# Products with v in float16 parts for the second piece of an attention and MLP kernel, with weight conversions queued two units earlier

## The chip, the cores and the metric

The kernel runs on one core of a Trainium2 chip. The metric is device time in microseconds (us) of one execution. Five engines with queues of their own work side by side: TensorE (PE) multiplies matrices out of the on-chip memory into accumulation banks, VectorE (DVE) and ScalarE (ACT) work element by element, GpSimd (POOL) does a little of that, and SyncE (SP) issues transfers (DMA). Each engine takes its instructions in the order of its queue. An instruction whose input isn't there holds up all that stands behind it.

## What is computed

The input is q, k and v for 2 batches, 8 heads, 768 positions and 64 dimensions a head. Attention keeps a window of 128 positions and 4 sinks at the start. Its output goes through a normalised two-layer network, and that through a gated mixing stage, which the change leaves alone.

```
scores = scale * q @ k.T                  # masked: first n_sink keys, or 0 <= pos_q - pos_k < window
a = exp(scores - max); a = a / sum(a)
x = a @ v                                 # heads side by side: (2, 768, 512)
xn = (x - mean) / sqrt(var + 1e-6) * g
x = x + relu(xn @ w_ch1) @ w_ch2          # w_ch1: 512 x 2048, w_ch2: 2048 x 512
theta = x @ w_theta                       # then cos, sin, two token mixes, a last product with relu
```

## The kernel before

The 1536 rows are cut into six pieces of two tiles of 128 rows (tiles, L482): pieces 0 to 2 are batch 0, pieces 3 to 5 batch 1. attn_fast (L275) is a generator that goes through pieces and heads, and stops (yield) between small groups of products, so that run (L820) can set other work of TensorE between them.

For each head softmax (L379) forms the scores (L273), subtracts from the mask with the row's extreme on DVE (L394), and takes the exponential with its sum on ACT (L397). A tile sees two blocks of 128 keys (its own and the one before) and, from the third tile of a batch on, 16 columns of sinks. For the product with v the weights must be transposed, and there are two ways. Pieces 0 and 1 (TURNED is 2) are transposed on TensorE, in float32: turn_w (L433) transposes the blocks into one bank, wp, and copies them out into wt, by ACT in even heads (L449), by DVE in odd ones (L447); turn_sinks (L452) transposes the sink columns of the next head into a free half of the bank pv, and DVE copies them to ws (L458); values (L460) multiplies with v in float32 (L477), one head after its transposes, and normalize (L494) scales the result out of pv into x. Bank pv is a single one here, and so is bank wp from unit 0 on. Later pieces split the weights into two float16 parts (send_w, L402: high part on ACT, rest on DVE), which a transfer transposes. With v in two float16 parts too, a block takes three products: high x high, high x low, low x high. Three groups of 16 rows stand in one product for the sinks.

v comes in two forms. whole_v (L200) loads a tile in float32 as it is, for pieces 0 and 1. split_v (L181) loads a tile to a buffer vr, of which there is one, writes the high part on ACT (L196, for the sinks' tile L190) and the rest on DVE (L198). The pool for v holds five tiles. load_v (L286) asks for a piece's tiles while the piece before is in work, but for piece 2 only at the end of piece 1.

The network runs in units: unit u is the 128 hidden rows of one block of weights, u modulo 16, for all pieces that take part. first (L641) is the product with w_ch1, then the relu on ACT (L651, from unit 8 on L674); second (L679) is the product with w_ch2 into acc (L696). Piece 0 starts at unit 0, piece 1 joins at unit 8. Units 0 to 7 use float32 (L649); from unit 8 on x and the weights are each split into two parts on ACT and DVE (L637, L638; x in norm_T, L625 and L626).

The weights come as 64-bit numbers. load_w12 (L569) loads the two blocks of unit f (512 KB each) and load64 (L546) makes float32 of each: L555 on DVE, L556 and L558 on ACT, L559 on DVE. There are four buffers for the raw numbers, so that the load of f waits for the conversion of f-2. Conversions of f=0 to 3 are placed in the first piece. For the others run has this loop, where `newest` and behind() put all that load_w12 gives to ACT behind the relu of unit u in ACT's queue:

```
while f < NF and f <= u + AHEAD[u >= OFF - 1]:
    self.newest = [self.relu[u]]
    with self.behind():
        self.load_w12(f)
```

With AHEAD (2, 3) f=4 stands behind the relu of unit 2, f=8 behind that of unit 6, f=9 and f=10 behind that of unit 7, f=11 behind that of unit 8. TensorE's order is the program's own (manual_schedule); the other queues are ordered at build time by a planner that works with estimated durations, and the first two pieces' transposes, products and normalisations have high priority in it. range_whole (L206) at the end of attention loads once more those tiles of v that were never split, for a check of their range.

Of the kernel before, what the change touches and what calls it, by code (L numbers as in the profile page):

```python
# [8 lines left out]
F32 = mybir.dt.float32  # L9
F32R = mybir.dt.float32r  # L10
F16 = mybir.dt.float16
# [10 lines left out]
NT = S // 128  # L22
# [30 lines left out]
AHEAD = (2, 3)  # L53
# [16 lines left out]
class Net:  # L70
# [110 lines left out]
    def split_v(self, b, t):  # L181
# [6 lines left out]
        if t == NT:  # L188
            o = p["v"].tile([128, DM], F16, tag="vk", name="vk", bufs=1)
            nc.scalar.activation(o, r, AF.Copy, scale=VSC)  # L190
            r, lo, hi = r[64:96], o[64:96], o[64:96]
            self.v3[b, t] = o
        else:
            o = p["v"].tile([128, 2, DM], F16, tag="v", name="v")
            hi, lo = o[:, 0], o[:, 1]
            nc.scalar.activation(hi, r, AF.Copy, scale=VSC)  # L196
            self.v3[b, t] = hi, lo
# [77 lines left out]
    def attn_fast(self, eng):  # L275
# [10 lines left out]
        def load_v(piece):  # L286
            if piece < NP:
                b, tiles = self.tiles(piece)
                if piece < TURNED:
                    for t in tiles:  # L290
                        self.whole_v(b, t)
                    return
# [6 lines left out]
        def turn():  # L299
# [3 lines left out]
            with ahead(piece):  # L303
                blocks = self.turn_w(pt, tiles, h)
            sinks = []
            if tiles[0]:
                p["ws"].append(p["ws"].pop(0))
                sinks = [p["ws"][-1][0:NSK, i] for i in range(PIECE)]
# [30 lines left out]
        for j, (piece, h) in enumerate(steps):  # L339
# [4 lines left out]
            if h == (3 if piece else V_NEXT) and piece != TURNED - 1:  # L344
                load_v(piece + 1)
            pt, st = yield from self.softmax(h, tiles, qk[piece, h])
# [4 lines left out]
            if piece < TURNED and h == H - 1:  # L351
# [8 lines left out]
                if piece == TURNED - 1:  # L360
                    load_v(piece + 1)
# [17 lines left out]
    def softmax(self, h, tiles, qk):  # L379
# [19 lines left out]
        self.inverse(st, PSC * VSC if qk[1] is not None else 1.0)  # L399
# [33 lines left out]
    def turn_w(self, pt, tiles, h):  # L433
# [7 lines left out]
        for x, (i, t) in enumerate(keys):  # L441
            c0 = (t + 1 - tiles[i]) * KW
            nc.tensor.transpose(ps[:, x * 128:(x + 1) * 128], pt[:, i, c0:c0 + 128], self.ident)  # L443
        wt = self.att["wt"].tile([128, m, 128], F32, tag="wt", name="wt")
        ps = ps[:, 0:m * 128].rearrange("p (m k) -> p m k", k=128)
# [6 lines left out]
    def turn_sinks(self, bank, pt, sinks):  # L452
# [5 lines left out]
        nc.vector.tensor_copy(self.att["ws"][-1][0:NSK], ps)  # L458

    def values(self, b, h, tiles, piece, blocks, sinks, st, after):  # L460
# [6 lines left out]
        for i in range(len(tiles)):  # L467
            if piece < TURNED:
                prods = [(a, self.whole[b, t][:, hc]) for (j, e, t), a in blocks.items() if j == i]
                if sinks:  # L470
                    prods.append((sinks[i], self.whole[b, 0][0:NSK, hc]))
            else:
                prods = [(a, v[:, hc]) for (j, e, t), a in blocks.items() if j == i for v in self.v3[b, t][:2 - e]]
                if sinks:
# [345 lines left out]
    def run(self, general):  # L820
# [27 lines left out]
        else:  # L848
# [6 lines left out]
            a["ws"] = [ws.tile([128, PIECE, 128], F32, name=f"ws{i}") for i in range(2)]  # L855
# [243 lines left out]
```

## Time and profile before

| | |
|---|---|
| runs shown | 617.91, 623.66, 625.28 us; median 623.66 |
| the profiled execution | 617.65 us, span 615.9 us |
| TensorE busy | 584.7 us, 95% |
| DVE, ACT, POOL busy | 408.5, 334.0, 60.1 us |
| granted clock of TensorE, mean | 0.983 |
| transfers | 56.4 MB, 32% of the DMA engines' time |

The profile is of one execution, and its own time (617.65 us) lies near the lowest of the runs. Busy time of TensorE counts from a matmul's start to its modelled end, and matmuls overlap; what a group of them costs on the path is read from the chain of waits. The granted clock is a share of the full 2.4 GHz. An idle time stands in brackets behind the instruction that ended it, with the engine and line that the profile takes for its cause.

### The profile page before, as it was taken

The numbers are of one execution on the slowest core, as the hardware profiler recorded it, in microseconds if no ns is written. First come the engines' busy times: TensorE is split into PE (matmuls) and PEld (weight loads), VectorE is DVE, ScalarE is ACT, GpSimd is POOL, SyncE is SP. The second block draws the span as 40 slices with busy tenths as digits, with TensorE's granted clock in tenths as the row PEclk, the third lists the DMA queues.
The fourth block names the chain that finished last, engine by engine and source line by source line (L and its number), as shares of the span: only waits on it lengthen the run. The fifth ranks groups of instructions, "written<-read, shape, count | busy, mean of one in ns | idle before, by whom it ended". The sixth has DMA issues, their size and how long they took to land.

```text
span 615.9 us, 9332 instructions
## 1 busy us (share of the span) xinstructions
PE 584.7 (95%) x3473; PEld 479.8 (78%) x3473; DVE 408.5 (66%) x925; ACT 334.0 (54%) x732; POOL 60.1 (10%) x53
## 2 busy tenths in 40 slices
PE   5969998899999999999999899999999899999996
PEld 3756666577777777777788678888999789999996
DVE  4763465889867776976775643367798789754262
ACT  3834563998755656655556633346676656532020
POOL 1000000000000000000021200001343332300100
PEclk9999997899999999999999989999999999999998
DMA  7641442789722533433312310000232322010112
GB/s 274 215 159 44 160 156 86 251 209 222 130 54 49 117 82 71 96 69 60 78 54 101 103 51 2 0 1 1 102 104 104 103 69 70 1 35 34 36 36 74
DMA packets 55367, 56.41 MB, mean 92 GB/s; under 512 B 40080, under 2 KB 43152, under 8 KB 55312
## 3 DMA queue, kind: packets, MB, share of 16 engines
q1 hardware_dynamic: 55312, 55.72, 32.0%
q8 instruction: 29, 0.48, 0.3%
q14 instruction: 26, 0.21, 0.1%
HBM read 43.12 MB, written 3.15 MB: 75 GB/s over the span
## 4 chain that ended last, share of the span: by engine, by line
PE 69%; DVE 13%; DMA 7%; ACT 6%; issue 2%; POOL 1%; SPq 0%; ACTq 0%; POOLq 0%
PE acc L696 19%; PE h L670 18%; PE s L273 9%; PE m L781 5%; PE f L812 5%; PE pv L477 5%; PE h L649 3%; DVE st L559 2%; DMA raw<-wtok 2%; DMA raw<-w 2%; PE th L740 2%; PE wp L443 2%; ACT st L558 1%; ACT raw L556 1%; DVE st L555 1%
## 5 line engine op out<-in xcount | busy, mean ns | idle before, releaser
L638 DVE TENSOR_TENSOR wl<-w,wh 128x512 fp32r<-128x512 f32 x96 | 69.0, 723 | 53.4 <-ACT wh L637 26.7
L637 ACT ACTIVATE wh<-w 128x512 fp32r<-128x512 f32 x96 | 59.9, 628 | 77.5 <-PE acc L696 44.0
L670 PE MATMUL h<-xT,wh 128*128 128x512 f32 (+1 forms) x384 | 96.8, 388 | 2.4 <-DVE w L555 2.4
L670 PEld LDWEIGHTS h<-xT,wh 128*128 128x128 f32 x384 | 67.1, 191 | 18.2 <-ACT xT L625 2.6
L696 PE MATMUL acc<-wh,hh 128*128 128x512 f32 x176 | 73.2, 416 | 0.0
L397 ACT ACTIVATE p<-p,st 128x272 f32<-128x272 f32 (+1 forms) x96 | 47.4, 494 | 43.7 <-DVE st L394 43.3
L696 PE MATMUL acc<-wl,hh 128*128 128x512 f32 x176 | 69.6, 395 | 0.0
L696 PE MATMUL acc<-wh,hl 128*128 128x512 f32 x176 | 69.5, 395 | 0.0
L394 DVE CUSTOM_DVE_ANT_0 p<-s,mask 128x272 f32<-128x272 f32 (+1 forms) x96 | 39.3, 411 | 29.7 <-PE s L273 28.9
L670 PE MATMUL h<-xT,wl 128*128 128x512 f32 (+1 forms) x192 | 48.8, 376 | 0.0
L696 PEld LDWEIGHTS acc<-wh,hh 128*128 128x128 f32 x176 | 33.5, 190 | 9.4 <-issue 1.2
L556 ACT ACTIVATE raw<-raw 128x512 f32<-128x512 f32 (+1 forms) x52 | 37.0, 715 | 6.5 <-DVE st L555 6.4
L670 PEld LDWEIGHTS h<-xT,wl 128*128 128x128 f32 x192 | 35.0, 191 | 6.8
L477 PE MATMUL pv<-v,wt 128*128 128x64 f16 (+1 forms) x472 | 38.2, 228 | 1.9 <-DVE x L494 1.9
L696 PEld LDWEIGHTS acc<-wh,hl 128*128 128x128 f32 x176 | 33.5, 190 | 7.8 <-DVE hl L675 0.3
L696 PEld LDWEIGHTS acc<-wl,hh 128*128 128x128 f32 x176 | 33.4, 190 | 6.0 <-DVE wl L638 0.4
L767 POOL TENSOR_TENSOR x<-xh,xl 128x512 f32<-128x512 f32 x12 | 19.3, 1607 | 131.1 <-DVE r L761 131.1
L597 POOL TENSOR_TENSOR rs<-rs,mhalf 128x2 f32<-128x2 f32 x6 | 4.8, 805 | 266.9 <-ACT rs L596 266.9
L675 DVE SCALAR_TENSOR_TENSOR hl<-h,hh 128x512 fp32r<-128x512 f32 (+1 forms) x48 | 30.7, 639 | 0.2 <-ACT hh L674 0.2
L273 PE MATMUL s<-raw 64*128 64x272 f32 (+1 forms) x64 | 24.1, 520 | 6.9 <-DMA raw<-qk 6.4
L558 ACT ACTIVATE st<-raw 128x768 uint16<-128x768 uint16 (+1 forms) x20 | 19.4, 971 | 18.6 <-DMA raw<-wtok 7.2
L674 ACT ACTIVATE hh<-h 128x512 fp32r<-128x512 f32 (+1 forms) x48 | 26.5, 552 | 5.5 <-PE h L670 5.5
(287 smaller groups left out, 1442.3 us busy)
## 6 DMA issues: line engine op xcount, KB each, us to landing
raw<-w SPq DMA_DIRECT2D x32, 512.0 KB, 4.3
raw<-wtok SPq DMA_DIRECT2D x12, 768.0 KB, 4.2
raw<-qk SPq DMA_DIRECT2D x16, 336.0 KB, 3.0
vr<-vt SPq DMA_DIRECT2D x14, 256.0 KB, 3.0
out_dram<-o SPq DMA_DIRECT2D x24, 128.0 KB, 1.7
raw<-qk SPq DMA_DIRECT2D x8, 272.0 KB, 4.0
raw<-wth SPq DMA_DIRECT2D x4, 512.0 KB, 3.3
raw<-wch SPq DMA_DIRECT2D x4, 512.0 KB, 3.3
```

Of the source, the lines that this page charges most:

```text
L273: self.nc.tensor.matmul(ps, q[:, c], k[:, k0:k0 + kn], start=j == 0, stop=j == len(prods) - 1)
L394: self.newest = [nc.vector.tensor_tensor_reduce(out=e, in0=ps[:, c0:WIN], in1=self.mask[min(t, 2)], scale=-0.125, scalar=3e38, op0=ALU.add ...
L397: nc.scalar.activation(e, e, AF.Exp, bias=st[:, 0, i:i + 1], scale=-1.0, accum_out=st[:, 1, i:i + 1])]
L477: nc.tensor.matmul(pv[:, i * D:(i + 1) * D], a, m, start=j == 0, stop=j == len(prods) - 1)
L556: nc.scalar.activation(hi.bitcast(F32), hi.bitcast(F32), AF.Copy, scale=2.0 ** -112)
L637: nc.scalar.activation(hi, r, AF.Copy)
L638: nc.vector.tensor_tensor(out=lo, in0=r, in1=hi.bitcast(F32), op=ALU.subtract)
L670: nc.tensor.matmul(ps[:, 0:n], a[:, k * 128:(k + 1) * 128], x[:, k, c], start=m == 0, stop=m == 11)
L675: nc.vector.scalar_tensor_tensor(out=hl, in0=ps[:, 0:n], scalar=0.0, in1=hh.bitcast(F32), op0=ALU.max, op1=ALU.subtract)
L696: nc.tensor.matmul(ps, a[:, c], w, start=m == 0 and n == 0, stop=m == NF - 1 and n == len(prods) - 1)
L781: nc.tensor.matmul(ps, z[i][e][:, c * 128:(c + 1) * 128], w[:, t], start=s == 0 and m == 0 and c % 2 == 0, stop=s == NT - 1 and m == 5 and ...
L812: nc.tensor.matmul(ps, self.w_last[k][e][:, c * 128:(c + 1) * 128], u[k][f], start=m == 0, stop=m == 11)
```

## The change

The second piece (piece 1) leaves the float32 way for its product with v. turn_w still transposes on TensorE, but writes two float16 parts out of bank wp: the high part on ACT, the rest on DVE, in every head. turn_sinks does the same for the sink columns. values makes three products for a block, as later pieces do, and three short ones (16 rows) for the sinks: high x high, high x rest of v, rest x high. For that the sinks' tile of v gets a second small tile, vl, with its rest in rows 0 to 31. load_v splits the tiles of piece 1 (1, 2, 3 and the sinks' tile) while piece 0 is in work, and asks for piece 2 (tiles 4 and 5 then) in head 3 of piece 1, not at its end. The factor in inverse follows. Piece 0 stays as it is.

AHEAD becomes (4, 4): f=4 stands behind the relu of unit 0, f=10 behind that of unit 6, f=11 behind that of unit 7, f=15 behind that of unit 11.

```diff
-AHEAD = (2, 3)
+AHEAD = (4, 4)
...
             nc.scalar.activation(o, r, AF.Copy, scale=VSC)
+            if b == 0:
+                self.vl = p["v"].tile([128, DM], F16, tag="vl", name="vl", bufs=1)
+                nc.vector.scalar_tensor_tensor(out=self.vl[0:32], in0=r[0:32], scalar=VSC, in1=o[0:32], op0=ALU.mult,
+                                               op1=ALU.subtract)
...
         def load_v(piece):
-                if piece < TURNED:
+                if piece == 0:
...
-                blocks = self.turn_w(pt, tiles, h)
+                blocks = self.turn_w(pt, tiles, h if piece == 0 else None)
...
-                sinks = [p["ws"][-1][0:NSK, i] for i in range(PIECE)]
+                sinks = [[p["ws"][-1][0:NSK, e, i] for e in range(2)] for i in range(PIECE)]
...
-            if h == (3 if piece else V_NEXT) and piece != TURNED - 1:
+            if h == (3 if piece else V_NEXT):
                 load_v(piece + 1)
...
-                if piece == TURNED - 1:
-                    load_v(piece + 1)
...
-        self.inverse(st, PSC * VSC if qk[1] is not None else 1.0)
+        self.inverse(st, PSC * VSC if tiles[0] or b else 1.0)
...
     def turn_w(self, pt, tiles, h):
+        if h is None:
+            wt = self.att["wt"].tile([128, 2 * m, 128], F16, tag="wt", name="wt")
+            nc.scalar.activation(wt[:, 0:m], ps, AF.Copy, scale=PSC)
+            nc.vector.scalar_tensor_tensor(out=wt[:, m:], in0=ps, scalar=PSC, in1=wt[:, 0:m], op0=ALU.mult,
+                                           op1=ALU.subtract)
+            return {(i, e, t): wt[:, e * m + x] for e in range(2) for x, (i, t) in enumerate(keys)}
...
     def turn_sinks(self, bank, pt, sinks):
-        nc.vector.tensor_copy(self.att["ws"][-1][0:NSK], ps)
+        ws = self.att["ws"][-1]
+        nc.scalar.activation(ws[0:NSK, 0], ps, AF.Copy, scale=PSC)
+        nc.vector.scalar_tensor_tensor(out=ws[0:NSK, 1], in0=ps, scalar=PSC, in1=ws[0:NSK, 0], op0=ALU.mult,
+                                       op1=ALU.subtract)
...
     def values(self, b, h, tiles, piece, blocks, sinks, st, after):
-            if piece < TURNED:
+            if piece == 0:
                 prods = [(a, self.whole[b, t][:, hc]) for (j, e, t), a in blocks.items() if j == i]
-                if sinks:
-                    prods.append((sinks[i], self.whole[b, 0][0:NSK, hc]))
             else:
                 prods = [(a, v[:, hc]) for (j, e, t), a in blocks.items() if j == i for v in self.v3[b, t][:2 - e]]
-                if sinks:
+                if sinks and piece < TURNED:
+                    prods += [(sinks[i][e], v[0:NSK, hc]) for e, v in (
+                        (0, self.v3[b, NT]), (0, self.vl), (1, self.v3[b, NT]))]
+                elif sinks:
                     prods.append((sinks[i], self.v3[b, NT][:, hc]))
...
-            a["ws"] = [ws.tile([128, PIECE, 128], F32, name=f"ws{i}") for i in range(2)]
+            a["ws"] = [ws.tile([128, 2, PIECE, 128], F16, name=f"ws{i}") for i in range(2)]
```

## Rows read from the trace of the kernel before

**Rows 1.** The page: busy time of TensorE, share, instructions

```profile
PE 584.7 (95%) x3473; PEld 479.8 (78%) x3473; DVE 408.5 (66%) x925; ACT 334.0 (54%) x732; POOL 60.1 (10%) x53
```

**Rows 2.** Stages: length, busy us (instructions) of each engine, granted clock, DMA share, GB/s

```profile
50.30:99.50 49.20, 46.47 (x225) 32.27 (x224) 24.83 (x75) 24.96 (x63) 0.00 (x0) 0.97 0.39 129
99.50:117.50 18.00, 15.64 (x58) 10.04 (x57) 14.74 (x40) 14.31 (x33) 0.83 (x1) 0.88 0.47 160
117.50:150.00 32.50, 32.48 (x186) 23.34 (x187) 29.82 (x82) 29.95 (x79) 0.00 (x0) 0.90 0.95 229
```

**Rows 3.** The same view in slices of 5 us (PE, PEld, DVE, ACT, POOL)

```profile
95.00:100.00 5.00, 3.60 (x13) 3.16 (x14) 1.93 (x5) 0.63 (x1) 0.00 (x0) 0.65 0.13 24
...
115.00:120.00 5.00, 2.61 (x8) 1.64 (x7) 4.47 (x12) 5.00 (x14) 0.00 (x0) 0.70 0.89 243
```

**Rows 4.** TensorE's timeline: its three waits from 45 to 130 us

```profile
90.12 0.66 PE L443 MATMUL wp<-ident,p 128*128 128x128 f32 x4 [0.85 <-ACT wt L449]
...
96.40 0.96 PE L477 MATMUL pv<-v,wt 128*128 128x64 f32 x4 [1.89 <-DVE x L494]
...
117.52 2.07 PE L670 MATMUL h<-xT,wh 128*128 128x512 f32 x4 [2.39 <-DVE w L555]
```

**Rows 5.** ACT's timeline: relu of unit 5, a head's copy, the second transposed x

```profile
86.88 0.37 ACT L651 ACTIVATE hh<-h 128x256 f32<-128x256 f32 x1
...
89.51 0.56 ACT L449 ACTIVATE wt<-wp 128x512 f32<-128x512 f32 x1
...
116.90 0.57 ACT L625 ACTIVATE xT<-tp 128x512 fp32r<-128x512 f32 x1
```

**Rows 6.** DVE's timeline: the conversion ahead of the last head's sinks

```profile
95.31 0.46 DVE L555 TENSOR_SCALAR w<-raw 128x512 uint16<-128x512 uint16 x1 [1.07 <-DMA raw<-w]
```

**Rows 7.** The chain in order of time: start, us on the chain, what

```profile
57.47 1.70 PE pv L477 x12
...
91.15 4.14 DMA raw<-w
...
96.40 3.24 PE pv L477 x12
99.64 3.71 PE h L649 x8
...
106.09 1.92 PE h L649 x8
...
117.53 2.07 PE h L670 x4
...
124.14 0.57 PE s L273 x3
...
134.17 1.14 PE h L670 x4
...
137.95 0.42 PE pv L477 x14
```

**Rows 8.** Groups by line, 50.3 to 99.5 us; last two: line 477, ns min/median/max

```profile
L449 ACT ACTIVATE wt<-wp 128x512 f32<-128x512 f32 x4 | 2.4, 588 | 2.1 <-PE wp L443 2.1
...
L447 DVE COPY wt<-wp 128x512 f32<-128x512 f32 x4 | 2.7, 679 | 0.9 <-PE wp L443 0.8
...
L458 DVE COPY ws<-pv 16x256 f32<-16x256 f32 x8 | 3.3, 410 | 6.9 <-PE pv L457 6.8
...
L555 DVE TENSOR_SCALAR w<-raw 128x512 uint16<-128x512 uint16 x8 | 3.7, 457 | 8.4 <-DMA raw<-w 8.4
...
L477 PE MATMUL pv<-v,wt x64: 219/275/475, 57.3 to 98.6; 128*128 128x64 f32 x64
...
L477 PE MATMUL pv<-v,ws x32: 270/318/471, 57.8 to 99.2; 16*128 16x64 f32 x32
```

**Rows 9.** Lines 196 and 198, the splitting of v: ns min/median/max

```profile
L196 ACT ACTIVATE v<-vr x9: 602/614/632, 19.1 to 253.7; 128x512 f16<-128x512 f32 x9
...
L198 DVE SCALAR_TENSOR_TENSOR v<-vr,v x9: 673/685/694, 19.8 to 254.9; 128x512 f16<-128x512 f32 x9
```

More of the change, by code (lines that the diff above doesn't have):

```diff
@@ L343, in attn_fast @@
             load(j + 2)
-            if h == (3 if piece else V_NEXT) and piece != TURNED - 1:
+            if h == (3 if piece else V_NEXT):
                 load_v(piece + 1)
-            pt, st = yield from self.softmax(h, tiles, qk[piece, h])
+            pt, st = yield from self.softmax(b, h, tiles, qk[piece, h])
             if piece < TURNED:
@@ L377, in attn_fast, with softmax @@
         self.range_whole()
-    def softmax(self, h, tiles, qk):
+    def softmax(self, b, h, tiles, qk):
         nc, p = self.nc, self.att
@@ L443, in turn_w @@
             nc.tensor.transpose(ps[:, x * 128:(x + 1) * 128], pt[:, i, c0:c0 + 128], self.ident)
+        ps = ps[:, 0:m * 128].rearrange("p (m k) -> p m k", k=128)
+        if h is None:
[4 more added lines that the diff above has]
+            return {(i, e, t): wt[:, e * m + x] for e in range(2) for x, (i, t) in enumerate(keys)}
         wt = self.att["wt"].tile([128, m, 128], F32, tag="wt", name="wt")
-        ps = ps[:, 0:m * 128].rearrange("p (m k) -> p m k", k=128)
         if h % 2:
```

## The prediction, made before the changed kernel was run

> **What bounds the kernel now.** I read the page's line of TensorE first, then the table of stages, then TensorE's own timeline with its waits, the chain of waits through the stage that the change touches, and last ScalarE's and VectorE's timelines around each wait. TensorE (PE) is busy for 95% of the span [rows 1], so a change pays where it takes instructions from PE or ends a time in which PE waits or runs at half clock. The second piece's attention runs from 50.3 to 99.5 us beside units 1 to 5 of the first piece's network. PE is busy there for 46.47 of 49.20 us, ScalarE (ACT) and VectorE (DVE) for about half of it each [rows 2]; so PE sets the pace, with idle time at the end. From 99.5 to 117.5 PE loses another 2.4 us, and in this stage and the next ACT is nearly full (29.95 of 32.50 us in the next) [rows 2]. The slices of 5 us show where the clock fell: 0.65 granted in 95 to 100, 0.70 in 115 to 120, in each right behind idle time of PE [rows 3]; the lower of its two levels is 1.2 GHz, the upper 2.4.
>
> PE has three waits here [rows 4]. At 90.12 the transposes wp of the last head wait 0.85 us for ACT, which copies the head before them out of the one wp bank: that copy (89.51) stands in ACT's queue behind the relu of 86.88 and the four conversions of weights that queue behind it [rows 5]. At 96.40 the last head's product with v waits 1.89 us: DVE must copy the sinks and scale the result before it, and stands in front of this on an L555 whose weights land only at 95.3 [rows 6]. At 117.52 unit 8's first product waits 2.39 us; the profile names an L555, but what it needs is the second transposed x from ACT (L625 at 116.90), behind a queue of conversions for f=9 and f=10, v and exponentials [rows 5].
>
> **The change part by part.** Sums are against the profiled execution, 617.65 us for a span of 615.9.
>
> *Products with v.* A head of the second piece now has 4 key blocks and 2 sinks in float32, which the chain shows as 12 records in 1.70 us. After it there are, per tile, 2 blocks x 3 float16 products and 3 short ones: 18 per head. Later pieces do such products already: 14 in 0.42 us, 0.030 each [rows 7]. A float16 product of 16 rows is not in the trace; in float32 the short one has a median of 318 ns and the long one 275 [rows 8], so I bound it at 0.030 x 318/275 = 0.035. 18 x 0.030 = 0.54 us (0.57 at the upper bound). A head saves 1.70 - 0.54 = 1.16 us; the last one, at half clock, takes 3.24 [rows 7] and would take 0.54 x 3.24/1.70 = 1.03, a saving of 2.2.
>
> The Trainium skill speaks against this term: "TensorE: Matmul & The Clock Gate", section "Back-to-back issue gap", has a stream of pairs of weight load and matmul at about 81 ns a matmul for 128 columns. By that, taken as an upper estimate for 64 columns, a head would cost 18 x 0.081 = 1.46 us and save only 0.24. The trace's 0.030 for this very form decides.
>
> *What of this stays.* For the first five heads the whole saving shortens the path, since PE is the bound: 5 x 1.16 = 5.8 us. For heads 5 and 6 I expect nothing. The last head's product starts 9.52 us behind the relu of 86.88, by a chain without PE: four conversions on ACT, L559, a load issued when its buffer comes free (4.14 us), L555, the copy of the sinks [rows 5 to 7]. After the change there are again conversions behind that relu (of f=9, not f=7) and again a load that they set free (f=11, not f=9), so I let the chain stand; what PE saves in heads 5 and 6, 2.3 us, becomes more waiting. The sinks now need an ACT pass and then a DVE pass where one DVE copy of 0.41 us was [rows 8]; only the DVE pass is behind the L555, with the same shape: 0 to 0.4, I take 0.3. Sum: 5.8 + 2.2 - 0.3 = 7.7 us gained.
>
> *More work on ACT and DVE.* wt was one copy, ACT 588 ns and DVE 679 ns in turn [rows 8]; now every head takes both, one behind the other, 1.27 instead of 0.63 us, and the wp bank is held that long. ACT gets half of 8 x 0.59 plus 8 sinks of at most 0.41: at most 5.6 us on 24.96; DVE gets half of 8 x 0.68, 2.7 us on 24.83 [rows 2, 8]. Both fit into 49.20 - 7.7 = 41.5 us, at 74% and 66%. Cover for it: a head's wp bank is wanted again only a head later, about 5 us with the shorter product. Where conversions sit in between the cover is gone. Bounds: 0 and 8 x 0.64 = 5.1 us; I take 0.9, near the lower end, since the one wait of this kind in eight heads is 0.85 [rows 4].
>
> *v is split earlier.* Tiles 1, 2, 3 and the sinks' tile are now converted in the first piece, tiles 4 and 5 once its buffers come free: before 44.6 us, five conversions more on ACT (0.614) and six on DVE (0.685, the added remainder of the sinks among them) [rows 9]. To 36 us PE is busy, and they hide. The two that come free with the first piece's last product meet its normalisation on DVE, where PE waits: 0 to 2 x 0.69 us; and two v loads fewer at the start could give back some tenths. I take 1.0 lost.
>
> *Weight conversions two units earlier.* f=4 and f=5 queue behind the relus of units 0 and 1, when ACT is idle, and one f stands behind the relu of unit 7, where two do now. Each f is four ACT passes, 2.6 us from relu to the next instruction [rows 5]. With v's tiles gone too (0.61 for L196 and L190 each), ACT has about 2.6 + 1.2 = 3.8 us less in front of the L625 of 116.90, so it comes at about 113.1, while PE has work to 115. The wait of 2.39 goes; what is late next is the low part of x on DVE, needed four matmuls later. With the wait the half clock goes: from 117.53 to 124.14 the chain has 6.61 us of products that take 3.78 in the next unit, from 134.17 to 137.95 [rows 7], so 2.83 more. Together 5.2 us. Loads are not late: a load needs the buffer of f-2, which is free two units before its conversion, and the one at 91.15 took 4.14 us [rows 7]. SP's queue holds the same weight loads in the same order, earlier by one or two units against v's and q/k's; POOL gets nothing. Bounds of this part: 0 (DVE holds the same place) and 5.2 + 1.79, if the half clock at 99.64 (3.71 us for 1.92) goes as well [rows 7].
>
> **Sum:** 7.7 - 0.9 - 1.0 + 5.2 = 11.0 us gained; the profiled execution would become 606.6 us. It lies 6.0 us below the median of the runs shown (623.66), near the lowest (617.91); I expect the same scatter and put the median half of that up: 609.6 us. The terms give 612.7 if the whole scatter returns.
>
> **The rivals.** All on the same footing (sum plus 3.0).
> - *All of PE's waits go.* For it: the 95.3 wait is one DMA landing late in DVE's queue; with f=11 wanted four units on, it could stand elsewhere. Against it: the load is still set free by the same relu. Then 8 x 1.16 + 1.54 (half clock in the last product) + 1.79 + 1.89 + 0.85 + 5.22 = 20.6 us gained, less 1.0: 601 us.
> - *ACT keeps unit 8 waiting.* For it: ACT is full from 115 to 120 [rows 3], nearly so to 150 [rows 2], and first passes only move. Against it: 3.8 us leave its queue. Then 7.7 - 1.9 = 5.8 gained: 615 us.
> - *The wp bank becomes the bound (the other side).* ACT's 2.6 us of conversions stand in front of a head's copy, then DVE's pass waits for an L555; in this stage these waited 8.4 us in all for weights [rows 8]. If each head's transposes wait for it, the saving of 9.3 is gone at 1.2 us a head, and over 2% slower (12.4 more) needs 2.7 us a head: ACT's block plus a pass of DVE, without the head of cover. At 3 us a head: 8 x 3 - 9.3 + 1.0 = 15.7 lost, 636 us. Against it: ACT and DVE have a quarter and a third of the time free.
> - *Short products are slow*: by the price of 1.46 us of pairs, if rows of later pieces don't carry over, 8 x 0.24 = 1.9 gained instead of 7.7: 615 us with the other terms.
>
> **How the numbers follow.** Forecast 0.42; all waits go 0.20; ACT keeps unit 8 waiting 0.25; the bank becomes the bound 0.08; slow short products 0.05. The forecast's own range is 604 to 615 (terms at their bounds by halves). The range reaches beyond the all-gone case by the scatter, 598 us, and over the two middle rivals, 621 us; the other side and a tail are left out. 2% is 12.5 us, about what a measurement of this kernel can tell from no change. A gain of 11.0 is just short of it: of the forecast I count 0.18 as over, with the all-gone case and a little of the rest 0.40; slower over 2% 0.07; within 0.53.
>
> **What would show it.** Right: pv of the second piece in about 0.54 us a head; that stage shorter by some 8 us; no wait of PE before unit 8 and a granted clock near 1.0 where it was 0.70; still a wait of 2 us or more before the last head's product, on an L555 or the sinks' low part. Wrong: waits of wp on wt in most heads (the bank); ACT's L625 as late behind the last transposes as now (unit 8); a start of the first unit more than 1.4 us later (v's splits).

## The result, and the profile after

The changed kernel takes 614.37 us in the median of four runs (613.16 to 614.99), the kernel before, run beside it, 624.27 (617.91 to 625.28). The ratio is 0.9899, with a 95% interval of 0.9858 to 0.9941: about 1.0% faster. This ratio is not the quotient of the two medians, which is 0.984. The forecast was 609.6 us and 2.3%. Profiled execution against profiled execution the forecast was 617.65 to 606.6, a gain of 11.0; measured is 613.93 (span 612.1), a gain of 3.7. The medians differ by more because of scatter: the runs of before spread over 7 us with the profiled one near the lowest, those of after over 2 us. The longer runs are those with the lower clock: among the runs of before beside e1 its mean is 0.965 in those of 624.5 to 625.7 us and 0.980 to 0.983 in those of 618.7 to 620.2 us.

Busy times of the page (after), to be held against [rows 1]:

```profile
PE 578.1 (94%) x3521; PEld 470.9 (77%) x3521; DVE 411.8 (67%) x930; ACT 338.7 (55%) x746; POOL 60.5 (10%) x53
```

TensorE lost 6.6 us of work (584.7 to 578.1), but the span lost only 3.8. So idle time came in. The stages (after; columns as in [rows 2]):

```profile
50.30:99.50 49.20, 42.56 (x269) 26.17 (x267) 32.80 (x90) 33.94 (x86) 0.00 (x0) 0.97 0.51 171
99.50:117.50 18.00, 18.00 (x83) 11.77 (x81) 14.59 (x41) 14.24 (x38) 0.69 (x1) 0.91 0.51 150
117.50:150.00 32.50, 31.97 (x209) 23.00 (x208) 30.22 (x89) 29.99 (x81) 0.00 (x0) 1.00 0.84 182
```

In the second piece PE is busy for 42.56 of 49.20 us, where it was 46.47. The stage from 99.5 lost its idle time, as forecast, but little of its half clock (0.88 to 0.91); the one from 117.5 lost its half clock (0.90 to 1.00) and has 0.5 us of idle time that it did not have. Where the time went is read by setting the same instruction of both traces side by side, the n-th product of a kind. After minus before, in us:

| instruction (its start before) | after − before | the stage's change |
|---|---|---|
| first product of unit 0 (44.63) | +1.96 | +1.96 |
| first scores behind it (50.29) | +2.62 | +0.66 |
| scores behind the second piece (105.43) | +0.42 | −2.20 |
| a product h behind unit 8's wait (126.34) | −4.63 | −5.05 |
| scores of a later piece (156.65) | −4.62 | 0.0 |
| a product h of the later units (407.05) | −3.38 | +1.24 |

So the start cost 2.6 where I took 1.0, the second piece gave 2.2 where I took 7.7 − 0.9 = 6.8, unit 8 gave 5.05 where I took 5.2, and 1.2 went where I looked for nothing. That last piece is one transfer of 768 KB: ScalarE waits for it in both kernels, 2.17 us before and 3.86 after. The same transfer reads 4.25 us from issue to landing in before's chain and 5.94 in after's. It is scatter: e3 below turns out to run the same instructions as the changed kernel, and there the transfer reads 4.43.

Inside the second piece the scores of its last head mark the place where the products with v of its first five heads are done, first before, then after:

```profile
83.72 1.18 PE L273 MATMUL s<-raw 64*128 64x272 f32 x4
```

```profile
84.50 1.18 PE L278 MATMUL s<-raw 64*128 64x272 f32 x4
```

TensorE's timeline (after), all its waits of over 0.25 us between 53 and 130 us; they answer to [rows 4]:

```profile
59.92 0.66 PE L446 MATMUL wp<-ident,p 128*128 128x128 f32 x4 [0.27 <-DVE wt L451]
60.97 0.35 PE L490 MATMUL pv<-v,wt 128*128 128x64 f16 x6 [0.39 <-DVE ws L469]
65.89 0.63 PE L446 MATMUL wp<-ident,p 128*128 128x128 f32 x4 [0.58 <-DVE wt L451]
83.25 0.35 PE L490 MATMUL pv<-v,wt 128*128 128x64 f16 x6 [0.46 <-DVE x L507]
92.95 1.08 PE L446 MATMUL wp<-ident,p 128*128 128x128 f32 x4 [3.75 <-DVE wt L451]
99.36 0.34 PE L490 MATMUL pv<-v,wt 128*128 128x64 f16 x6 [1.20 <-DVE x L507]
```

There is no wait before unit 8 any more. The wait of wp for the copy of the head before it grew from 0.85 to 3.75, and the last head's product still waits 1.20. Four short waits, 1.70 us in all, came in where the kernel before had none. The first of them has its cause in VectorE's queue (after): the second pass of wt stands behind a conversion whose weights land late.

```profile
58.84 0.46 DVE L568 TENSOR_SCALAR w<-raw 128x512 uint16<-128x512 uint16 x1 [1.80 <-DMA raw<-w]
59.19 0.68 DVE L451 SCALAR_TENSOR_TENSOR wt<-wp,wt 128x512 f16<-128x512 f32 x1
```

ScalarE's timeline (after) shows why wt is late for the long wait; it answers to [rows 5]:

```profile
87.81 0.76 ACT L251 ACTIVATE hi<-raw 128x672 fp32r<-128x672 f32 x1 [2.73 <-DMA raw<-qk]
88.48 0.36 ACT L664 ACTIVATE hh<-h 128x256 f32<-128x256 f32 x1
88.74 0.66 ACT L569 ACTIVATE raw<-raw 128x512 f32<-128x512 f32 x1
89.30 0.76 ACT L571 ACTIVATE w<-raw 128x512 uint16<-128x512 uint16 x1
89.93 0.64 ACT L569 ACTIVATE raw<-raw 128x512 f32<-128x512 f32 x1
90.46 0.77 ACT L571 ACTIVATE w<-raw 128x512 uint16<-128x512 uint16 x1
91.09 0.50 ACT L400 ACTIVATE p<-p,st 128x272 f32<-128x272 f32 x1
91.50 0.19 ACT L400 ACTIVATION_READ_ACCUMULATOR p<-p,st 128x1 f32 x1
91.59 0.58 ACT L450 ACTIVATE wt<-wp 128x512 f16<-128x512 f32 x1
```

Three things stand in one queue in front of the copy at 91.59. First comes a split of q and k (L251), which waits 2.73 us for its transfer; then the relu of unit 5 (L664), then four conversions of weights, 2.6 us from relu to exponential. Before, the two splits of these heads came at 77.21 and 82.68, the second after a wait of 0.29. Now the first comes at 81.19, behind ScalarE's new passes, VectorE's half of it ends at 83.96, only that frees the buffer, and the transfer for the second goes out at 83.99. Behind the long wait TensorE runs at half clock for a while. Slices of 5 us (after):

```profile
90.00:95.00 5.00, 2.05 (x6) 1.53 (x7) 3.29 (x6) 4.66 (x13) 0.00 (x0) 0.80 0.82 245
95.00:100.00 5.00, 3.80 (x36) 1.86 (x36) 2.67 (x7) 0.67 (x2) 0.00 (x0) 0.84 0.09 35
100.00:105.00 5.00, 5.00 (x21) 3.49 (x18) 3.11 (x8) 1.44 (x4) 0.00 (x0) 0.67 0.15 52
115.00:120.00 5.00, 5.00 (x22) 3.49 (x23) 4.51 (x15) 5.00 (x18) 0.00 (x0) 1.00 0.85 209
```

The granted clock from 115 to 120 is 1.00 where it was 0.70 [rows 3]; from 100 to 105 it is still 0.67.

### The profile page after: what moved, and what is told of

It is laid out like the page before. It is cut to its first block, busy times and chain, and to the rows that moved or that the text cites. A ratio compares the mean times of both kernels' runs of the same rounds, so it can differ in the third digit from the quotient of the medians.

```text
span 612.1 us, 9452 instructions
## 1 busy us (share of the span) xinstructions
PE 578.1 (94%) x3521; PEld 470.9 (77%) x3521; DVE 411.8 (67%) x930; ACT 338.7 (55%) x746; POOL 60.5 (10%) x53
## 4 chain that ended last, share of the span: by engine, by line
PE 58%; DVE 17%; ACT 12%; DMA 8%; issue 3%; POOL 1%; SPq 0%; ACTq 0%; DVEq 0%; POOLq 0%
PE acc L709 18%; PE h L683 16%; PE s L278 6%; PE m L794 5%; PE f L825 5%; PE pv L490 3%; ACT raw L569 3%; DMA raw<-wtok 2%; DVE st L572 2%; DMA raw<-w 2%; PE th L753 2%; PE h L662 2%; ACT st L571 1%; ACT w L571 1%; DVE st L568 1%
## 5 line engine op out<-in xcount | busy, mean ns | idle before, releaser
L683 PE MATMUL h<-xT,wh 128*128 128x512 f32 (+1 forms) x384 | 95.2, 383 | 0.2 <-ACT wh L650 0.2
L490 PE MATMUL pv<-v,wt 128*128 128x64 f16 (+1 forms) x504 | 33.6, 215 | 2.3 <-DVE x L507 1.7
L688 DVE SCALAR_TENSOR_TENSOR hl<-h,hh 128x512 fp32r<-128x512 f32 (+1 forms) x48 | 30.6, 638 | 0.2 <-ACT hh L687 0.2
L572 DVE SCALAR_TENSOR_TENSOR w<-raw,w 128x512 int32<-128x512 int32 x32 | 21.9, 688 | 12.9 <-ACT w L571 9.9
```

The source lines that it names most:

```text
L490: nc.tensor.matmul(pv[:, i * D:(i + 1) * D], a, m, start=j == 0, stop=j == len(prods) - 1)
L572: nc.vector.scalar_tensor_tensor(out=dst, in0=hi, scalar=3, in1=dst, op0=ALU.logical_shift_left, op1=ALU.bitwise_or)
L683: nc.tensor.matmul(ps[:, 0:n], a[:, k * 128:(k + 1) * 128], x[:, k, c], start=m == 0, stop=m == 11)
```

## The experiments

All on one core, against runs of the kernel before on the same chip. Line numbers shift by up to six where lines were added. The table sets the same five instructions beside before (profiled execution minus before's, us); the texts after it say what each run was for. Two of them, e3 and e11, turned out to run the very instructions of another kernel (see there) and serve as repeats.

| kernel | median us | ratio [95%] | 50.29 | 105.43 | 126.34 | 156.65 | 407.05 |
|---|---|---|---|---|---|---|---|
| after | 614.37 | 0.9899 [0.9858, 0.9941] | +2.62 | +0.42 | −4.63 | −4.62 | −3.38 |
| e1 parts only | 618.55 | 0.9947 [0.9911, 0.9982] | +1.07 | −3.59 | −2.90 | −1.12 | +0.61 |
| e2 AHEAD only | 612.43 | 0.9821 [0.9775, 0.9866] | +0.19 | −0.61 | −5.42 | −6.00 | −4.49 |
| e3 late v (runs as after) | 615.86 | 0.9882 [0.9828, 0.9935] | +0.78 | +0.83 | −3.86 | −3.35 | −2.71 |
| e4 short ones last | 614.20 | 0.9841 [0.9793, 0.9890] | +1.65 | +1.05 | −3.30 | −3.11 | −1.20 |
| e5 two banks | 613.08 | 0.9819 [0.9763, 0.9876] | +2.84 | +0.72 | −3.34 | −3.68 | −3.34 |
| e6 wt on DVE | 615.65 | 0.9857 [0.9796, 0.9918] | +1.21 | +0.01 | −4.74 | −4.91 | −2.69 |
| e8 v on POOL | 612.83 | 0.9814 [0.9756, 0.9871] | +2.37 | −0.52 | −4.66 | −4.95 | −3.54 |
| e10 q, k later | 612.77 | 0.9821 [0.9764, 0.9878] | +1.79 | −2.24 | −6.46 | −5.98 | −7.28 |
| e11 = e3 + e10 (runs as e10) | 612.81 | 0.9836 [0.9780, 0.9892] | +0.88 | −1.90 | −6.92 | −6.57 | −5.35 |
| e12 = e8 + e10 | 611.74 | 0.9820 [0.9762, 0.9878] | +0.84 | −3.16 | −7.33 | −7.39 | −6.03 |
| e13 = e12, none behind relu 5 | 609.91 | 0.9806 [0.9731, 0.9881] | +1.32 | −8.31 | −11.41 | −9.79 | −8.15 |
| e14 none behind relu 5 | 614.92 | 0.9872 [0.9804, 0.9939] | +1.08 | −1.73 | −3.08 | −2.81 | −2.40 |

Most of the intervals overlap; what tells the kernels apart is the columns to the right, each from one profiled execution. How far these scatter is seen from the two pairs that run the same instructions, after with e3 and e10 with e11: they differ by 1.84 and 0.91 us at 50.29, by 0.41 and 0.34 at 105.43, by 0.77 and 0.46 at 126.34, by 1.27 and 0.59 at 156.65, and by 0.67 and 1.93 at 407.05.

**The two halves of the change apart.** e1 is the changed kernel with the old AHEAD, e2 the kernel before with the new one.

```diff
-AHEAD = (4, 4)
+AHEAD = (2, 3)
```

> The float16 parts with the old queueing, AHEAD (2, 3). Theory A (the parts themselves cost what was lost: a start 2.6 us late by v's splits, and a wp bank held while ACT is late): the first unit still starts at 46 to 47 us, the transposes of the last heads still wait 2 us or more for wt, and since f=9 and f=10 are again both behind the relu of unit 7, two to five of the 5 us won at unit 8 are given back; the profiled execution 615 to 619 us. Theory B (pulling conversions two units forward is what jams ACT in the second piece, and the wait at unit 8 went because v's splits left): the second piece takes 4 us less than in the changed kernel and unit 8 keeps its gain; 608 to 611 us.

> The kernel before with AHEAD (4, 4) and nothing else. Theory A: the start is that of before (44.6 us, within 0.5), no wait of wp above 1.5 us, the wait of 2.4 us at unit 8 and the half clock behind it go at least by half; 612 to 615 us, no slower than the changed kernel. Theory B: a jam of ACT in the second piece costs 2 us or more and unit 8 still waits, since v's splits are still queued there; 617 to 620 us.

e2 alone has at least the whole gain (612.43; its profiled execution is 4.6 us under before's, that of the full change 3.7; the intervals overlap, so that it has more is not shown). It takes unit 8's wait away and costs nothing elsewhere. e1 gives 4.66 us in the second piece (from +1.07 to −3.59), and loses it again at units 8 and 9. TensorE's timeline of e1, its four longest waits from 85 to 125 us:

```profile
90.59 1.12 PE L446 MATMUL wp<-ident,p 128*128 128x128 f32 x4 [4.66 <-DVE wt L451]
96.91 0.34 PE L490 MATMUL pv<-v,wt 128*128 128x64 f16 x6 [1.20 <-DVE x L507]
113.06 1.19 PE L683 MATMUL h<-xT,wh 128*128 128x512 f32 x4 [1.53 <-ACT xT L638]
122.87 0.39 PE L278 MATMUL s<-hi 64*128 64x272 f32 x1 [2.67 <-DVE st L397]
```

The scores at 122.87 wait for VectorE, where a conversion whose weights landed 0.63 us late and three more passes come first:

```profile
120.59 0.46 DVE L568 TENSOR_SCALAR w<-raw 128x512 uint16<-128x512 uint16 x1 [0.63 <-DMA raw<-w]
120.94 0.84 DVE L252 TENSOR_TENSOR lo<-raw,hi 128x672 fp32r<-128x672 f32 x1
...
122.38 0.42 DVE L397 CUSTOM_DVE_ANT_0 p<-s,mask 128x272 f32<-128x272 f32 x1
```

So with weights converted late, a faster second piece only arrives earlier at the next wait. The long wait of wp on wt is there without the new AHEAD too (4.66): it belongs to the float16 parts. Of the short waits of the changed kernel e1 has only that of 0.46 (at 79.99), so the others come of the parts and the new AHEAD together.

**The start.** e3 is meant to ask for v's tiles 4 and 5 at the end of the second piece again, as before; e8 moves the second pass of v's split from VectorE to GpSimd.

```diff
-            if h == (3 if piece else V_NEXT):
+            if h == (3 if piece else V_NEXT) and piece != TURNED - 1:
...
+                if piece == TURNED - 1:
+                    load_v(piece + 1)
```

```diff
+        if b == 0 and t < NT:
+            nc.gpsimd.tensor_scalar(out=r, in0=r, scalar1=VSC, scalar2=0.0, op0=ALU.mult, op1=ALU.add)
+            nc.gpsimd.tensor_tensor(out=lo, in0=r, in1=hi, op=ALU.subtract)
+            return
```

> The changed kernel, but tiles 4 and 5 of v are again asked for at the end of the second piece. Theory A: their two conversions leave DVE's queue between 36 and 45 us, so the first unit starts 0.7 to 1.4 us earlier than in the changed kernel (46.59); they come back ahead of unit 8 and cost up to 1.5 us there; in all 612 to 615 us. If the late start has another cause (the sinks' tile and vl, or the order of the loads), the first unit starts at 46.3 to 46.9 as in the changed kernel.

> The changed kernel with the second part of the split of v's tiles of the first batch on GpSimd (a multiplication and a subtraction) instead of VectorE. Theory A (the 1.96 us by which the first unit starts later than before are VectorE's splits of v and of the sinks' rows, queued ahead of the first unit's normalisation): the first unit starts 0 to 1.0 us later than before instead of 1.96, and the second piece's start comes as much earlier. Theory B (the late start comes from the transfers of v, which now come before the first unit's weights): it starts 1.7 to 2.3 us later as in the changed kernel. Of the end, by A 613 to 614, by B 614 to 615.

e3 does not test this. The request moved in the program, but the planner brings the loads forward again: in the traces every engine's instructions are those of the changed kernel, one by one and in the same order (the fifth and sixth load of v go out at 33.62 and 38.70, in the changed kernel at 35.05 and 40.40). So e3 is a second execution of the changed kernel. That its first unit starts in theory A's range (45.54) is scatter. Nine executions have the changed kernel's queues of all engines up to 50 us (after, e1, e3 to e6, e10, e11, e14); their first unit starts 0.91 to 2.07 us later than before, 1.5 in the mean, and their column of 50.29 reads +0.78 to +2.84.

e8 leaves the first unit at +1.95, against theory A; e12 and e13, the same up to there, have it at +1.13 and +1.34. So in the start its edit makes no difference that stands out from the scatter. In e8 the normalisation (L616, 41.55; L612 at 41.50 in after, L599 at 39.59 before) is just as late with v's passes gone from VectorE, because a conversion ahead of it now waits for weights. VectorE's timeline of e8:

```profile
40.37 0.93 DVE L572 TENSOR_SCALAR w<-raw 128x512 uint16<-128x512 uint16 x1 [0.77 <-DMA raw<-w]
```

SyncE's timeline has a likely reason, which no run tests: before, four loads of weights were issued in a row from 30.94 on; in e8 and in after a load of v stands between the second and the third (in e8 at 34.61, the third going out at 35.95). What e8 does change lies later. In e8, e12 and e13 the second pass of wt stands ahead of the late conversion (in e8 at 57.42 and 59.26), and the time from the scores of 50.29 to those of 83.72 is 2.8 to 2.9 us shorter than before, in the other kernels with both parts of the change 0.3 to 1.8.

**The products themselves.** e4 puts the short products of both tiles behind all the long ones, so that TensorE changes between 128 and 16 rows twice in a head instead of four times.

```diff
-                    prods += [(sinks[i][e], v[0:NSK, hc]) for e, v in (
+                    short += [(i, sinks[i][e], v[0:NSK, hc]) for e, v in (
...
+        for x, (i, a, m) in enumerate(short):
+            nc.tensor.matmul(pv[:, i * D:(i + 1) * D], a, m, start=False, stop=x == len(short) - 1)
```

> The changed kernel, with the short products of both tiles behind the long ones of both, so that TensorE changes between 128 and 16 rows twice in a head's product with v, not four times. If each change costs about 0.095 us (the trace of the changed kernel: 0.028 from product to product, 0.12 where the rows change), a head's product takes 0.64 us for 0.83, and at most 1.5 us are won, less where a wait follows: 612 to 614 us. If the products are simply slower than later pieces' ones, it stays at 0.83.

TensorE's timeline of one head, first after, then e4:

```profile
66.41 0.33 PE L490 MATMUL pv<-v,wt 128*128 128x64 f16 x6
...
66.72 0.19 PE L490 MATMUL pv<-vl,ws 16*128 16x64 f16 x1
66.75 0.19 PE L490 MATMUL pv<-vk,ws 16*128 16x64 f16 x1
66.87 0.35 PE L490 MATMUL pv<-v,wt 128*128 128x64 f16 x6
...
67.22 0.19 PE L490 MATMUL pv<-vk,ws 16*128 16x64 f16 x1
67.34 0.39 PE L466 MATMUL pv<-ident,p 128*16 128x128 f32 x2
```

```profile
66.95 0.51 PE L492 MATMUL pv<-v,wt 128*128 128x64 f16 x12
...
67.46 0.22 PE L495 MATMUL pv<-vk,ws 16*128 16x64 f16 x2
...
67.67 0.39 PE L466 MATMUL pv<-ident,p 128*16 128x128 f32 x2
```

A head's products take 67.34 − 66.41 = 0.93 us to the next kind of work after, and 0.72 in e4 (before: 62.78 to 64.58, 1.80). Products of one kind follow each other at 0.03 us; from the last short one to the first long one it is 0.12 (66.75 to 66.87), from a short one to the transposes the same (67.22 to 67.34). So a change of the rows in use costs about 0.09 more than a step, four times a head. e4 saves 0.21 a head by that, 1.7 us over eight, and nothing arrives: the second piece ends at +1.05, with longer waits of wp (1.78 us at 60.46 and 4.73 at 93.44). The time per product was not what decided the end.

**The wait of wp.** e5 gives wp a second bank, e6 moves the first pass of wt from ScalarE to VectorE, e10 puts the split of q and k that waits at 87.81 behind the second piece's last exponential.

```diff
-        self.sbanks, self.vbanks, self.wbanks = [sb, ab[2]], [vb], [ab[3]]
+        self.sbanks, self.vbanks, self.wbanks = [sb, ab[2]], [vb], [ab[3], hb]
```

```diff
-            nc.scalar.activation(wt[:, 0:m], ps, AF.Copy, scale=PSC)
+            nc.vector.tensor_scalar(out=wt[:, 0:m], in0=ps, scalar1=PSC, scalar2=None, op0=ALU.mult)
```

```diff
-                    qk[piece, h] = qk[piece, h + 1] = self.split_qk(piece, h // 2, eng)
+                    with self.tc.issue_after(self.soft) if j == TURNED * H + 2 else ExitStack():
+                        qk[piece, h] = qk[piece, h + 1] = self.split_qk(piece, h // 2, eng)
```

> The changed kernel with a second PSUM bank for the transposes of the weights (wp), which otherwise wait until both passes of wt have read the one bank. Theory A (the bank, held while ScalarE is late, is what the second piece lost): TensorE's waits at wp for VectorE's wt, 4.6 us in the changed kernel (3.75 at 92.95), go to under 1 us, some of them come back as a wait of pv for wt itself (about 1.4 us, since relu and four conversions still stand ahead of wt's copy on ScalarE), and the end of the second piece is 1 to 3 us earlier than in the changed kernel (there 0.42 us later than before). Theory B (ScalarE's queue alone decides, whichever bank): the wait moves whole to pv, the end of the second piece moves by under 0.7 us. Time by A 612.0 to 613.5, by B 614 to 614.5.

> The changed kernel with the first pass of wt, the high part, on VectorE instead of ScalarE, so that ScalarE's late split of q and k and its four conversions no longer stand ahead of it. Theory A (ScalarE's lateness holds the bank): the wait of wp at 92.95 (3.75 us) falls by 2 to 3 us, and the second piece ends 1.5 to 3 us earlier than in the changed kernel; VectorE has some 0.6 us a head more, which the stretch's 33.94 us of 49.20 leave room for. Theory B (VectorE becomes the late engine in its place, as it does the exponentials' other half, the normalisation and the second pass): the waits of wp for wt stay at 4 us or more or come earlier, and the second piece ends no earlier. Time by A 611.5 to 613, by B 614 to 617.

> The changed kernel with ScalarE's second split of q and k of the next piece put behind the last exponential of the second piece, so that ScalarE no longer waits 2.73 us at 87.81 for that transfer with the relu of unit 5, four conversions and wt's copy queued behind it. Theory A (that wait is what makes wt late): the wait of wp at 92.95 (3.75 us) falls under 1.5 us, the relu of unit 5 comes 1.5 to 2.7 us earlier, and the second piece ends 1.5 to 3 us earlier than in the changed kernel. Theory B (the conversions themselves, four behind the relu, are what makes it late): the wait falls by under 1 us, the second piece ends within 0.7 us of the changed kernel's. Time by A 611.5 to 613, by B 613.7 to 615.

The longest wait of wp in each, from TensorE's timelines of e5, e6 and e10 in this order:

```profile
92.59 0.44 PE L446 MATMUL wp<-ident,p 128*128 128x128 f32 x2 [2.94 <-ACT p L400]
```

```profile
90.83 1.20 PE L446 MATMUL wp<-ident,p 128*128 128x128 f32 x4 [2.34 <-ACT p L400]
```

```profile
92.10 1.12 PE L448 MATMUL wp<-ident,p 128*128 128x128 f32 x4 [2.93 <-DVE wt L453]
```

With a second bank or with wt on the other engine the transposes wait for their input instead, the exponentials p, which stand in the same queue of ScalarE. The wait moved to another cause and is still 2.94 and 2.34 long, and the second piece gives no more than in the changed kernel (2.1 us from +2.84 to +0.72, 1.2 from +1.21 to +0.01). So the bank alone is not the cause, against theory A of e5 (its wait of 2.94 is followed by one of 0.55), and VectorE in ScalarE's place is no better. In e10 the wait is still 2.93 and the relu comes 0.86 us earlier (87.62), both short of theory A, and yet the piece ends 2.66 us earlier than in the changed kernel (3.07 than in e3). Its earlier start has no part in that, since wp waits 1.07 us at 59.89 where the changed kernel waited 0.27. The long wait gave 0.8 of it; much of the rest is the clock. Slices of 5 us, e10:

```profile
90.00:95.00 5.00, 2.90 (x7) 1.87 (x8) 3.78 (x8) 4.36 (x12) 0.00 (x0) 0.67 0.70 215
95.00:100.00 5.00, 3.80 (x44) 2.45 (x44) 3.02 (x9) 1.00 (x2) 0.00 (x0) 0.99 0.20 65
100.00:105.00 5.00, 5.00 (x22) 3.36 (x21) 4.53 (x14) 3.78 (x8) 0.70 (x1) 1.00 0.24 68
```

From 100 to 105 PE is busy throughout in both, at 1.00 against 0.67: 5 x 0.33 = 1.65 us of full-clock work.

**Together, and without the conversions.** e11 joins e3 and e10, e12 joins e8 and e10. e13 is e12 with no conversions behind the relu of unit 5 (that f goes behind the relu of unit 6, with f=10); e14 is the changed kernel with that edit alone.

```diff
-            while f < NF and f <= u + AHEAD[u >= OFF - 1]:
+            while f < NF and f <= u + AHEAD[u >= OFF - 1] - (u == 5):
```

> The two edits of e3 and e10 together: v's tiles 4 and 5 asked for at the end of the second piece's predecessor, and the second split of q and k behind the piece's last exponential. Theory A (two separate losses: the early transfers of v start the first unit late, and the transfer of q and k holds ScalarE in the last heads; the second swallows what the first gives, which is why e3 alone ended the second piece no earlier): the first unit starts 0.5 to 1.2 us later than before, the second piece ends 2.8 to 4.2 us earlier than before, beyond e10's 2.24. Theory B (e10's 2.24 is what the supply of weights allows, whatever the start): it ends 1.9 to 2.6 us earlier than before. Time by A 610.5 to 612, by B 612.3 to 613.5.

> The two edits of e8 and e10 together: the second part of the split of v's tiles on GpSimd, and the second split of q and k behind the last exponential. Theory A (e8's gain inside the second piece and e10's are separate): the second piece ends 2.6 to 3.6 us earlier than before. Theory B (both remove the same wait of the last heads): it ends 1.9 to 2.5 us earlier, as with e10 alone. Time by A 611.5 to 612.5, by B 612.5 to 613.3.

> The kernel of e12 with no conversions behind the relu of unit 5; its unit of weights comes behind the relu of unit 6, together with that one's own. Theory A (the wait of 2.9 us that wp's transposes still have in e10 to e12 is the four conversions, 2.6 us of ScalarE between the relu and the exponentials): the wait falls under 0.8 us, and as TensorE then stands idle less, its clock stays up, so that the second piece ends 4.5 to 7 us earlier than before (e12: 3.16); some 1 to 3 us of it may be given back at units 9 and 10, whose weights come later. Time by A 608 to 611. Theory B (VectorE's exponentials and second pass are next in line, or the late weights take it all back): the second piece ends under 4.2 us earlier, or the lead after unit 9 is under 7.4; time 611.5 to 614.

> The changed kernel with that one edit: no conversions behind the relu of unit 5. ScalarE's wait for q and k (2.73 us) stays. Theory A (the transfer and the conversions add up): the wait of wp falls from 3.75 to between 0.9 and 1.8 us, the second piece ends 1.5 to 4 us earlier than in the changed kernel, as much as with the transfer taken out (e10: 2.66). Theory B (one of the two alone holds wp, the other hides behind it): the wait stays over 2.7 us, the end moves by under 1 us. Time by A 611 to 613, by B 613.5 to 615.

Since e3's edit leaves the queues as they are, e11 runs e10's instructions, one by one, and tests neither of its theories (its request, too, stands at the end of the second piece itself). It starts its second piece 0.9 us earlier than e10 and ends it no earlier (−1.90): the wait of wp is 2.93 again, and its clock from 90 to 100 is lower (0.53 and 0.79). e12 came out by theory A, −3.16. e13 against e12 settles it: one edit lies between them, both take 30.6 us from the scores of 50.29 to those of 83.72, and from there to the end of the piece e12 takes 20.2 and e13 14.6. e13's ScalarE, its TensorE, and its slices:

```profile
85.33 0.39 ACT L670 ACTIVATE hh<-h 128x256 f32<-128x256 f32 x1 [2.57 <-PE h L668]
85.61 0.51 ACT L405 ACTIVATE p<-p,st 128x272 f32<-128x272 f32 x1
86.02 0.19 ACT L405 ACTIVATION_READ_ACCUMULATOR p<-p,st 128x1 f32 x1
86.11 0.58 ACT L456 ACTIVATE wt<-wp 128x512 f16<-128x512 f32 x1
```

```profile
87.48 0.66 PE L452 MATMUL wp<-ident,p 128*128 128x128 f32 x4 [0.60 <-DVE wt L457]
92.20 0.34 PE L496 MATMUL pv<-v,wt 128*128 128x64 f16 x6 [1.20 <-DVE x L513]
```

```profile
85.00:90.00 5.00, 4.40 (x41) 2.72 (x40) 3.24 (x9) 3.44 (x10) 0.00 (x0) 1.00 0.24 74
90.00:95.00 5.00, 3.80 (x42) 2.98 (x42) 2.38 (x9) 1.00 (x2) 0.00 (x0) 1.00 0.17 59
95.00:100.00 5.00, 5.00 (x22) 3.13 (x21) 4.53 (x12) 4.84 (x10) 0.69 (x1) 1.00 0.50 138
```

From relu to wt's copy it is 0.78 us instead of 3.11, the wait of wp is 0.60, the clock stays at 1.00 in these slices, and the second piece goes from +1.32 to −8.31: 9.6 us gained, more than e13's expectation and more than the prediction's 6.8. Not all of it is the float16 parts' doing. Eight heads at 0.87 us less make 7.0; the rest goes with the half clock that the kernel before has at the end of this stage (0.65 from 95 to 100 [rows 3]) and that is gone here, and no run clears the queues with the float32 products left in, which might end that too. Some 1.6 us are given back between 126 and 157, as expected, though I did not follow by which waits; the median is 609.91. e14 shows that both obstacles count: without the conversions, but with ScalarE's wait for q and k (3.06 us there), wp still waits 1.74 at 90.90 and the piece ends at −1.73, 2.15 us earlier than in the changed kernel (its earlier start went into a wait of wp of 1.76 at 59.87). Then unit 8 gives only 1.35 us (from −1.73 to −3.08), since TensorE waits there again (0.74 us at 110.27, 1.12 at 115.47, 1.64 at 122.68), and the kernel is no faster than the changed one.

e13 is the fastest kernel of the study by its median and by its trace. Its interval overlaps e2's, so the times alone don't show that it is worth more than AHEAD alone; the traces of one execution each speak for it, by 3.8 us at 156.65, where repeats differ by 0.6 and 1.3.

## Why the prediction was off

- *Weight conversions earlier: right.* Forecast 5.2 us, measured 5.05, and 4.81 in e2 (from −0.61 to −5.42). The second transposed x (L638) comes at 114.12 where [rows 5] had 116.90 and I took 113.1; wait and half clock are gone. "Loads are not late" did not hold: at 58.84 the conversion on VectorE waits 1.80 us for its weights, and the second pass of wt with it. The rival that ScalarE keeps unit 8 waiting is out.
- *A head's products: the mechanism right, the term mis-sized.* I took 18 x 0.030 = 0.54 us; measured 0.93 to the next kind of work, so 0.87 saved and not 1.16. The step that failed is that a short product was priced as one more step of the stream, without the change of rows before and after it: 18 x 0.03 + 4 x 0.09 = 0.90. Over the five heads that I counted that is 1.5 us of the 4.6 that are missing. The Trainium skill ("TensorE: Matmul & The Clock Gate", section "Back-to-back issue gap") spoke for 81 ns a product of 128 columns; the traces show 29 to 30, and the rival of slow short products is out.
- *"PE sets the pace": the step that failed, with the 0.9 us set for the wait of wp.* The saving reaches the end only while ScalarE and VectorE keep up. I let their work stand at its busy share (74% and 66% of the stage) and asked whether it fits; what decides is the order in their queues. The last head's scores stand behind the products of the first five heads (83.72 before, 84.50 after). From the scores of 50.29 (52.91 after) to these it took 33.43 us before and 31.59 after: 1.84 gained (0.73 in e3) where I took 5.8. The products gave 5 x 0.87 = 4.4 of it, and 2.5 went back, 1.70 in the four short waits. From here to the end of the piece 0.36 were gained (in e3 0.78 lost) where I took 2.2 − 0.3 = 1.9: the product of head 6 (92.34 before, 96.84 after) slipped 4.6 us against that of head 5, 2.9 by the longer wait of wp and 1.7 by half clock behind it. So of the 4.6 us missing from a term of 6.8 some 1.5 are the price of a product, 1.6 the waits of the first five heads beyond the 0.9, and 1.5 the last three heads.
- *The bank.* I had named it as the other side with 0.08, priced for every head; wp waited in three heads, 4.6 us in all where 0.85 had been, and it did not make the kernel slower. The cause was also misnamed: a second bank does not help (e5). For the long wait the runs show the cause, a split that waits for a transfer, a relu and four conversions ahead of wt's copy in ScalarE's queue (e10, e12 with e13, e14); for the first short one the trace shows a late conversion ahead of wt in VectorE's queue, and no run was made for it alone.
- *The last head's chain.* I let a wait of 2 us or more stand before its product, tied to the relu of unit 5 and an L555. The L555 is out of it; 1.20 us of waiting are left, for the sinks' two passes and the scaling behind them, and e13 has the same 1.20. In its place came the wait of wp. The sum of both waits went from 2.74 us [rows 4] to 4.95.
- *v split earlier.* Forecast 1.0. The changed kernel's scores behind unit 0 come 2.6 later, and its first unit 1.96, which I had named as a sign of being wrong; but in nine executions with the same queues up to there the scores come 0.8 to 2.8 later, 1.55 in the mean, so the size is not shown to be far off. With v's passes on GpSimd three kernels read +0.84 to +2.37. Its step "they hide" looked at ScalarE and VectorE only; what also moves is the load of weights that stands behind a load of v in SyncE's queue. No run separates the two, since e3's edit moved no load. Little of the start reaches the end: after and e3 start their second piece 1.84 apart and end it 0.41 apart.
- *Scatter.* I put half of before's 6 us between profile and median on top. The changed kernel's median lies 0.4 above its profiled execution. The two forecasts do not fit together either: 609.6 is 14.1 us under the median of before, more than the 2% that a gain of 11.0 was said to fall just short of. And the 636 us of the bank's rival leave out the 5.2 us of unit 8; with them it is 631.

## What to carry to other kernels

A bound that has slack by busy share can still be the bound by queue order: before taking PE's saving as path, follow the queue of each engine that feeds it through the one stretch where it is fullest, transfers included, at the new and faster pace. Work for later (a split, a conversion) that waits for its data ahead of work for now costs its whole wait, and moving it behind the last urgent instruction is worth more than a second buffer for what it holds up. Try the parts of a change alone: here one line gave all of the gain that was measured, and the stage of the other part gained 9.6 us only after the queues around it were mended. And look in the trace whether an edit moved anything: a planner that orders the queues can undo it, as in e3, and then the run is a repeat, which is worth having for the scatter alone.

## What the runs showed of the hardware

- A change between products of 128 rows and of 16 costs about 0.09 us on top of the 0.03 from product to product. The Trainium skill ("TensorEngine Tiling (Array Packing)", section "Key Properties") says that a change of tiling mode drains TensorE; it gives no figure, and that these two shapes are two modes is not shown here.
- A wait of PE can cost more than its length. Behind the 3.75 us at 92.95 the slices of the changed kernel read 0.84 and 0.67, and PE is busy throughout from 100 to 105 at that lower figure; in e13, whose longest wait in this stretch is 1.20, all read 1.00. It need not: behind a wait of 3.53 us at 349.58 in e10 the clock reads 1.00 from 350 to 355, behind one of 3.52 at 349.55 in e2 it reads 0.50. The 2.8 us between their last columns come from there.
- The same load of 768 KB, in the same place of the program, took 5.94 us in the changed kernel and 4.43 in e3, which runs the same instructions, and 4.34 and 5.42 in the pair e10 and e11.
